# Attention with two MLPs on one core: normalising the value products instead of the exponentials

## The chip, the cores and the metric

One core of a Trainium2 chip runs the whole program. The metric is the device time of one execution in microseconds (us). Engines are named as in the profile: PE (TensorE; PEld its weight loads), DVE (VectorE), ACT (ScalarE), POOL (GpSimd), SP (the engine that issues most transfers).

## The reference

Gated causal attention for 2 batches, 8 heads, 576 positions and 64 columns a head; then a mixture of four experts for all tokens with given probabilities; then a gated MLP.

```python
scores = scale * np.matmul(q, k.transpose(0, 1, 3, 2))
cum = np.cumsum(log_f, axis=-1)
decay = cum[:, :, :, None] - cum[:, :, None, :]
scores = np.where(causal, -1000000000.0, scores + decay)
scores = scores - np.max(scores, axis=-1, keepdims=True)
attn = np.exp(scores)
attn = attn / (np.sum(attn, axis=-1, keepdims=True) + 1e-09)
return np.matmul(attn, v).astype(np.float32)
...
for e in range(E):
    h = np.maximum(x @ w1[e], 0.0)
    out += p[:, e:e + 1] * (h @ w2[e])
...
h = x @ w_in
g = h * (1.0 / (1.0 + np.exp(-1.702 * h)))
return (g @ w_out).astype(np.float32)
```

## The kernel before

The tokens are cut into four chunks: chunk 0 is the first 256 positions of batch 0, chunk 1 its last 320, chunks 2 and 3 the same of batch 1. Attention makes a chunk's 512 columns in four pairs of heads; a chunk of finished columns (x) then goes through the experts, each in two halves, and the MLP. Matmuls of the experts run on a high part (rounded, fp32r) and a low part (the rest): weights are split into `whi` and `wlo`, activations into `xh` and `xl`, and three products are summed.

The attention of a chunk runs over units. In chunk 0 (called plain) a unit is one head with both of its tiles of 128 queries, in plain fp32; in the other chunks it is one tile of 128 queries (or the last 64) for both heads of a pair, with split keys and queries. There are 8 units in chunk 0, 12 in chunk 1 (three a pair), and 8 and 12 in chunks 2 and 3, 40 in all. `attention()` is a generator that emits one step at each pull; a step emits stage by stage: the scores of unit i and their maximum, the exponential and the normalisation of unit i-1, the transposes of unit i-2, and, where a pair has ended, the value product and the splitting of its output at three units behind.

- `emit_max` (L411) adds the decay to the scores, writes them to `e` in SBUF on DVE and takes the row's extreme `mx`. `emit_exp` (L444) is ACT's exponential in place, with the row's sum in `sm`.
- `emit_norm` (L451) adds 1e-9 and takes the reciprocal on DVE (one or two columns, L454 and L455), and multiplies each tile of exponentials by it on POOL (L457, 72 instructions).
- `emit_tr` (L460) transposes `e` on PE into PSUM (L475); ACT, or DVE in chunk 0, copies the result to `ph`.
- `emit_pv` (L489) multiplies the values with `ph` into PSUM, the two heads of a pair in lanes 0 to 63 and 64 to 127 (L505). `emit_x2` (L507) rounds that to `xh` on ACT and subtracts to `xl` on DVE (L514).

Keys, queries and values of a pair are loaded by `load_heads` (L319), one pair ahead; POOL rounds and subtracts them (L337, L338, L346, L347) three units before they are used, and adds the mask to broadcasts of the cumulated decay, `cb` and `cbs` (L349 on). Their pools have three buffers each.

While attention goes on, the main loop takes expert work for the chunks that are done, and pulls attention steps between groups of matmuls so that a chunk is ready when it is needed. `emit_first` does the first layer of chunk 0 as its columns come. The instructions are emitted in program order, and the scheduler of the language, which models time, sets the final order on each engine; engines then run their instructions strictly in order. After the last attention step `begin_late` (L269) closes the attention's pools, and DVE converts the MLP's weights (`mlp_convert`) beside the experts.

Of the kernel before, what the change touches and what calls it, by code (L numbers as in the profile page):

```python
# [15 lines left out]
NT = B * S  # L16
# [17 lines left out]
def attn_moe_mlp(ctx: ExitStack, tc: tile.TileContext, qk0, qk1, qk2, v0, vp, fg, dp, wa_moe, wb_moe, wa_mlp, wb_mlp, outT):  # L34
# [8 lines left out]
    def pool(name, bufs, space=None, scope=ctx):  # L43
        kw = {} if space is None else {"space": space}
        return scope.enter_context(tc.tile_pool(name=name, bufs=bufs, **kw))

    def f(ap):
        return ap.bitcast(F32)
# [32 lines left out]
    att_scope = ctx.enter_context(ExitStack())  # L81
    ac = pool("ac", 1, scope=att_scope)
    hi_p = pool("hi", 2, scope=att_scope)
    qhi_p = pool("qhi", 3, scope=att_scope)
    kq_p = pool("kq", 3, scope=att_scope)
    v_p = pool("v", 3, scope=att_scope)
    cb_p = pool("cb", 4, scope=att_scope)
    cbs_p = pool("cbs", 2, scope=att_scope)
    e_p = pool("e", 3, scope=att_scope)
# [159 lines left out]
        dpb[e] = t  # L249

    def load_probabilities():
        raw = const.tile([128, NT // 32], F32, name="dpraw")
        nc.sync.dma_start(out=raw, in_=dp)
        return raw

    def make_probabilities(raw):

        out = const.tile([128, 4, NT // 128], F32, name="dpn")
        s = const.tile([128, NT // 128], F32, name="dps")
        v = raw.rearrange("p (j e) -> p e j", e=4)  # L260
        nc.gpsimd.tensor_add(s, v[:, 0], v[:, 1])
        for e in (2, 3):
            nc.gpsimd.tensor_add(s, s, v[:, e])
        nc.gpsimd.tensor_scalar(out=s, in0=s, scalar1=1e-9, scalar2=1.0, op0=ALU.add, op1=ALU.mult)
        nc.vector.reciprocal(out=s, in_=s)
        nc.gpsimd.tensor_mul(out, v, s.unsqueeze(1).to_broadcast([128, 4, NT // 128]))
        nc.sync.dma_start(out=dpT.rearrange("e (p j) -> p e j", p=128), in_=out)
# [51 lines left out]
    def load_heads(p, h0):  # L319

        cs, b, s0 = p
        st = pairs[p, h0] = {}
        src = (qk2 if b else qk1)[h0 // 2]
        st["kq"] = kq_p.tile([128, KW], F32, tag="kq", name="kq")
        nc.sync.dma_start(out=st["kq"], in_=src[:, :KW])
        for i, c in enumerate(cs):
            st["q", c] = kq_p.tile([128, QW], F32, tag="qr", name="qr")
            nc.sync.dma_start(out=st["q", c], in_=src[:, KW + i * QW:KW + i * QW + QW])
        st["vd"] = v_p.tile([128, 5, 2, D], F32, tag="vd", name="vd")
        nc.sync.dma_start(out=st["vd"], in_=vp[b * H // 2 + h0 // 2].rearrange("p (t g d) -> p t g d", t=5, g=2))  # L330

# [119 lines left out]
    def emit_norm(c, u):  # L451
        e, sm, todo = sc[c, u]
        k = len(todo)
        nc.vector.tensor_scalar(out=sm[:, 1, :k], in0=sm[:, 0, :k], scalar1=1e-9, scalar2=None, op0=ALU.add)  # L454
        nc.vector.reciprocal(out=sm[:, 0, :k], in_=sm[:, 1, :k])  # L455
        for i, (q0, off, w, _) in enumerate(todo):
            nc.gpsimd.tensor_scalar(out=e[:, off:off + w], in0=e[:, off:off + w], scalar1=sm[:, 0, i:i + 1],  # L457
                                    scalar2=1.0, op0=ALU.mult, op1=ALU.mult)

    def emit_tr(c, u):  # L460

        hs, tiles = u
        s0 = CH[c][1]
        e, sm, todo = sc.pop((c, u))
        for h in hs:
            if (c, h) not in ph_of:
                ph_of[c, h] = pt_p.tile([128, 4, SB], F32, tag="ph", name="ph")
        for k, (q0, off, w, _) in enumerate(todo):
            o = q0 - s0
            nk = (w + 127) // 128  # L470

            for k0, k1 in [(0, min(nk, 4))] + [(4, 5)] * (nk > 4):
                pt = ps_t.tile([128, 512], F32, tag="t", name="t")
                for i in range(k0, k1):
                    nc.tensor.transpose(pt[:, 128 * (i - k0):128 * (i - k0) + 128], e[:, off + 128 * i:off + 128 * i + 128], ident)  # L475
                cols = pt[:, :128 * (k1 - k0)].rearrange("p (i q) -> p i q", q=128)
                for j, h in enumerate(hs if w == S else hs[k:k + 1] if len(hs) > 1 else hs):
                    r = 64 if w == S else 128
                    ph = ph_of[c, h]
                    ph = ph[:, 3:4, 0:64] if k0 else ph[:, 0:k1, o:o + r]  # L480
                    if plain(c) and k1 == 2:
                        nc.vector.tensor_copy(ph, cols[:, :, j * r:(j + 1) * r])
                    else:
                        round_act(ph, cols[:, :, j * r:(j + 1) * r])
# [22 lines left out]
    def emit_x2(c, h):  # L507
        n = CH[c][2]
        if h % 2 == 1:
            k = h // 2  # L510
            x = xf.pop((c, k))[:, :n]
            x_made[0] += 1
            round_act(xh[c][:, k, :], x)
            nc.vector.tensor_sub(xl[c][:, k, :], x, f(xh[c][:, k, :]))  # L514

    STAGES = dict(scores=0, max=0, exp=1, norm=1, tr=2, pv=3, x2=3)
    L_X2 = STAGES["x2"]
# [5 lines left out]
    def attention():  # L523
# [17 lines left out]
        for i in range(len(seq) + L_X2 + 1):  # L541
# [5 lines left out]
                prep_queries(*k)  # L547
            for k in new:
                prep_cum(*k)
            for k in names:  # L550
                j = i - STAGES[k]
                if k in per_unit:
# [268 lines left out]
```

## Time and profile before

| | |
|---|---|
| median of 3 runs | 731.88 us (731.81 to 733.29) |
| the profiled execution's own time | 733.77 us |
| its span in the trace | 732.0 us, mean granted clock 0.998 |
| PE busy | 710.5 us, 97% |
| DVE busy | 457.1 us, 62% |
| POOL busy | 295.1 us, 40% |
| ACT busy | 266.7 us, 36% |

The shares over the whole span hide that the program has stages: attention for chunk 0 alone at first, then attention beside experts, and from some 222 us on experts and MLP without attention. They are read by stretches of the span. PE's busy time counts a matmul from its start to a modelled end, so a waiting matmul can look busy; the time of the weight loads (PEld) is the second view of the same engine. A chain of waits is followed backward from its last instruction, and its shares say on which engine's work the end of the stretch waited.

### The profile page before, as it was taken

How to read it: one execution, taken by the hardware profiler on the slowest of the kernel's cores; microseconds unless marked ns; L12 is line 12 of the kernel's file. 1: busy time of each engine (PE TensorE's matmuls, PEld its weight loads, DVE VectorE, ACT ScalarE, POOL GpSimd, SP SyncE). 2: the span in 40 equal slices, each digit the busy share in tenths (PEclk: the TensorE clock that was granted, in tenths of full speed). 3: DMA queues.
4: the chain of work that ended last, by engine and by line, in shares of the span. 5: the costliest groups of instructions: out<-in, count | busy, mean ns of one | idle time of the engine just before them, and what ended most of it. 6: DMA issues, size and time to landing. Idle time of an engine off the chain costs nothing.

```text
span 732.0 us, 11991 instructions
## 1 busy us (share of the span) xinstructions
PE 710.5 (97%) x4488; PEld 681.7 (93%) x4488; DVE 457.1 (62%) x1023; ACT 266.7 (36%) x629; POOL 295.1 (40%) x377
## 2 busy tenths in 40 slices
PE   4988999999999999999999999999999999999998
PEld 3577889999999999999998999999999999999997
DVE  4765767577748999999999542345962124424422
ACT  4445655566642233222221221223354433333320
POOL 5997896774422022332232432232462222222220
PEclk9999999999999999999999999999999999999999
DMA  8866744332125555454344200000100000000012
GB/s 269 248 194 210 213 162 137 118 103 87 59 90 193 154 193 160 162 173 117 114 144 115 87 30 30 1 1 1 58 0 1 1 1 1 1 0 1 1 44 86
DMA packets 31225, 68.81 MB, mean 94 GB/s; under 512 B 3224, under 2 KB 4768, under 8 KB 31168
## 3 DMA queue, kind: packets, MB, share of 16 engines
q1 hardware_dynamic: 31120, 68.01, 29.6%
q8 instruction: 35, 0.57, 0.3%
q14 instruction: 22, 0.18, 0.1%
q10 hardware_dynamic: 48, 0.05, 0.0%
HBM read 65.62 MB, written 2.41 MB: 93 GB/s over the span
## 4 chain that ended last, share of the span: by engine, by line
PE 84%; POOL 7%; DMA 5%; issue 2%; DVE 1%; SPq 1%; ACT 0%; POOLq 0%; DVEq 0%
PE m L625 39%; PE m L581 39%; PE s L408 2%; POOL e L457 2%; PE x L505 2%; DMA kq<-in_qk_dram 2%; PE t L475 2%; DMA qr<-in_qk_dram 2%; POOL klo L338 1%; POOL qlo L347 1%; POOL cb L360 1%; DMA kd<-fr 1%; POOL cb L363 1%; POOL khi L51 1%; POOL qhi L51 1%
## 5 line engine op out<-in xcount | busy, mean ns | idle before, releaser
L641 POOL TENSOR_TENSOR acc<-acc,tmp 128x384 f32<-128x384 f32 (+3 forms) x112 | 111.9, 1010 | 237.4 <-DVE tmp L639 237.0
L625 PE MATMUL m<-hh,wlo 128*128 128x384 f32 (+2 forms) x640 | 127.7, 320 | 0.9 <-DVE wlo L165 0.9
L625 PE MATMUL m<-hh,whi 128*128 128x384 f32 (+2 forms) x640 | 128.4, 320 | 0.0
L625 PE MATMUL m<-hl,whi 128*128 128x384 f32 (+2 forms) x640 | 128.3, 319 | 0.0
L581 PE MATMUL m<-xh,whi 128*128 128x384 f32 (+2 forms) x624 | 125.7, 321 | 2.2 <-POOL whi L51 2.2
L581 PE MATMUL m<-xh,wlo 128*128 128x384 f32 (+2 forms) x624 | 125.4, 321 | 0.0
L581 PE MATMUL m<-xl,whi 128*128 128x384 f32 (+2 forms) x624 | 125.1, 320 | 0.0
L54 ACT ACTIVATE whi<-wst 128x512 fp32r<-128x512 f32 x103 | 64.8, 630 | 117.6 <-PE m L581 65.9
L625 PEld LDWEIGHTS m<-hh,whi 128*128 128x128 f32 x640 | 106.0, 189 | 1.7 <-issue 0.8
L625 PEld LDWEIGHTS m<-hh,wlo 128*128 128x128 f32 x640 | 105.8, 189 | 1.7 <-DVE wlo L165 1.6
L581 PEld LDWEIGHTS m<-xh,whi 128*128 128x128 f32 x624 | 103.7, 188 | 3.2 <-POOL whi L51 2.5
L625 PEld LDWEIGHTS m<-hl,whi 128*128 128x128 f32 x640 | 106.2, 189 | 0.2
L165 DVE TENSOR_TENSOR wlo<-wst,whi 128x512 fp32r<-128x512 f32 x112 | 90.4, 810 | 25.1 <-ACT whi L54 12.6
L581 PEld LDWEIGHTS m<-xl,whi 128*128 128x128 f32 x624 | 104.0, 188 | 0.2
L581 PEld LDWEIGHTS m<-xh,wlo 128*128 128x128 f32 x624 | 103.8, 188 | 0.3 <-DVE wlo L165 0.2
L616 POOL TENSOR_TENSOR hl<-tmp,hh 128x384 fp32r<-128x384 f32 x48 | 49.1, 1025 | 133.2 <-ACT hh L54 133.2
L607 ACT ACTIVATE hh<-m 128x384 fp32r<-128x384 f32 (+2 forms) x112 | 48.8, 437 | 116.1 <-PE m L581 115.0
L608 DVE SCALAR_TENSOR_TENSOR hl<-m,hh 128x384 fp32r<-128x384 f32 (+2 forms) x112 | 54.8, 492 | 32.3 <-ACT hh L607 32.2
L639 DVE TENSOR_TENSOR tmp<-m,dpb 128x384 f32<-128x384 f32 (+2 forms) x80 | 40.8, 511 | 34.3 <-PE m L625 28.3
L614 DVE TENSOR_TENSOR tmp<-m,sg 128x384 f32<-128x384 f32 x48 | 26.6, 554 | 54.2 <-ACT sg L613 54.2
L448 ACT ACTIVATE e<-e,mx 128x128 f32<-128x128 f32 (+4 forms) x72 | 42.0, 584 | 43.1 <-DVE mx L434 39.3
L457 POOL TENSOR_SCALAR e<-e,sm 128x128 f32<-128x128 f32 (+4 forms) x72 | 46.1, 650 | 21.7 <-DVE sm L455 17.1
(93 smaller groups left out, 771.7 us busy)
## 6 DMA issues: line engine op xcount, KB each, us to landing
wst<-in_wa_moe_dram SPq DMA_DIRECT2D x28, 512.0 KB, 4.6
wst<-in_wb_moe_dram SPq DMA_DIRECT2D x28, 512.0 KB, 4.0
mst<-in_wa_mlp_dram SPq DMA_DIRECT2D x16, 512.0 KB, 3.5
mst<-in_wb_mlp_dram SPq DMA_DIRECT2D x16, 512.0 KB, 3.8
cb<-cumd SPq DMA_DIRECT2D x16, 256.0 KB, 6.1
qr<-in_qk_dram SPq DMA_DIRECT2D x12, 256.0 KB, 3.7
kq<-in_qk_dram SPq DMA_DIRECT2D x8, 352.0 KB, 7.0
vd<-in_vp_dram SPq DMA_DIRECT2D x8, 320.0 KB, 3.7
```

The lines of the kernel that those rows point to most:

```text
L54: nc.scalar.activation(out=out, in_=in_, func=AF.Copy)
L165: sub = nc.vector.tensor_sub(lf, raw, f(hf))
L448: nc.scalar.activation(out=e[:, off:off + w], in_=e[:, off:off + w], func=AF.Exp, scale=-1.0, bias=mx, accum_out=sm[:, 0, k:k + 1])
L457: nc.gpsimd.tensor_scalar(out=e[:, off:off + w], in0=e[:, off:off + w], scalar1=sm[:, 0, i:i + 1], scalar2=1.0, op0=ALU.mult, op1=ALU.mult)
L581: nc.tensor.matmul(p[:, :n], lhsT=w[:, k, :], rhs=x[c][:, k, :], start=(j == 0 and k == 0), stop=(j == 2 and k == 3))
L607: nc.scalar.activation(out=hh[:, g, :n], in_=p[:, :n], func=AF.Relu)
L608: nc.vector.scalar_tensor_tensor(out=hl[:, g, :n], in0=p[:, :n], scalar=0.0, in1=f(hh[:, g, :n]), op0=ALU.max, op1=ALU.subtract)
L614: nc.vector.tensor_mul(t[:, :n], p[:, :n], s[:, :n])
L616: nc.gpsimd.tensor_sub(hl[:, g, :n], t[:, :n], f(hh[:, g, :n]))
L625: nc.tensor.matmul(p[:, :n], lhsT=w[:, k, :], rhs=x[:, k, :n], start=(j == 0 and k == 0), stop=(j == 2 and k == 3))
L639: nc.vector.tensor_mul(t[:, :n], p[:, :n], d)
L641: nc.gpsimd.tensor_add(a, a, t[:, z])
```

## The change

The exponentials are no longer multiplied by their reciprocal sums. Instead `emit_norm` writes each reciprocal, broadcast over 64 columns for each head, into a tile `rec`. With the last transposes of a pair, `emit_rec` transposes `rec` on PE into the same PSUM tile, so that every lane of a head holds the reciprocals along the queries, and ACT copies them to `rt`, which has one buffer. `emit_x2` multiplies the value product by `rt` on DVE into `xt`, and splits that; the subtraction to `xl` goes from DVE to POOL for chunks 1 to 3. Values are loaded by a function of their own at the pair's first unit. Keys and values have two buffers instead of three, and the small tiles of the probabilities live in a temporary.

```diff
+    xt_p = pool("xt", 2, scope=att_scope)
+    rec_p = pool("rec", 2, scope=att_scope)
...
-    v_p = pool("v", 3, scope=att_scope)
+    v_p = pool("v", 2, scope=att_scope)
...
-        st["kq"] = kq_p.tile([128, KW], F32, tag="kq", name="kq")
+        st["kq"] = kq_p.tile([128, KW], F32, tag="kq", name="kq", bufs=2)
...
+    def load_values(p, h0):
+
+        b = p[1]
+        st = pairs[p, h0]
         st["vd"] = v_p.tile([128, 5, 2, D], F32, tag="vd", name="vd")
...
     def emit_norm(c, u):
         e, sm, todo = sc[c, u]
         k = len(todo)
+        h = u[0][0]
+        if (c, h // 2) not in rec:
+            rec[c, h // 2] = rec_p.tile([128, 3, 2, 64], F32, tag="rec", name="rec")
+        r = rec[c, h // 2]
+        r = r[:, :2, h % 2, :] if plain(c) else r[:, (todo[0][0] - CH[c][1]) // 128]
         nc.vector.tensor_scalar(out=sm[:, 1, :k], in0=sm[:, 0, :k], scalar1=1e-9, scalar2=None, op0=ALU.add)
-        nc.vector.reciprocal(out=sm[:, 0, :k], in_=sm[:, 1, :k])
-        for i, (q0, off, w, _) in enumerate(todo):
-            nc.gpsimd.tensor_scalar(out=e[:, off:off + w], in0=e[:, off:off + w], scalar1=sm[:, 0, i:i + 1],
-                                    scalar2=1.0, op0=ALU.mult, op1=ALU.mult)
+        nc.vector.reciprocal(out=r, in_=sm[:, 1, :k].unsqueeze(2).to_broadcast([128, 2, 64]) if k == 2 else
+                             sm[:, 1, 0:1].unsqueeze(2).to_broadcast([128, 2, 64]))
+
+    rec, rcp = {}, {}
+
+    def emit_rec(c, h, pt, o):
+
+        r = rec.pop((c, h // 2))
+        n = CH[c][2]
+        for j in range(0, n, 128):
+            nc.tensor.transpose(pt[:, o + j:o + j + 128], r[:, j // 128].rearrange("p g d -> p (g d)"), ident)
+        t = rcp[c, h // 2] = xt_p.tile([128, SB], F32, tag="rt", name="rt", bufs=1)
+        round_act(t[:, :n], pt[:, o:o + n])
+        if n > 256:
+            round_act(t[64:, 256:n], pt[64:, o + n:o + n + 64])
...
+                if k + 1 == len(todo) and hs[-1] % 2 and k1 == nk and q0 + 128 >= s0 + CH[c][2]:
+                    emit_rec(c, hs[0], pt, 128 * (k1 - k0))
...
-            x = xf.pop((c, k))[:, :n]
+            p, r = xf.pop((c, k)), rcp.pop((c, k))
             x_made[0] += 1
+            x = xt_p.tile([128, SB], F32, tag="xt", name="xt")[:, :n]
+            nc.vector.tensor_mul(x, p[:, :n], r[:, :n])
             round_act(xh[c][:, k, :], x)
-            nc.vector.tensor_sub(xl[c][:, k, :], x, f(xh[c][:, k, :]))
+            (nc.vector if plain(c) else nc.gpsimd).tensor_sub(xl[c][:, k, :], x, f(xh[c][:, k, :]))
...
+            for k in nxt:
+                if first[k] == i:
+                    load_values(*k)
```

POOL's order when the first units of chunk 0 are on their way, before (`kq` and `qr` are the raw keys and queries of the first pair of chunk 1, `e` the exponentials of chunk 0):

```order
L51 TENSOR_SCALAR khi<-kq 128x704
L457 TENSOR_SCALAR e<-e,sm 128x128
L457 TENSOR_SCALAR e<-e,sm 128x256
L51 TENSOR_SCALAR qhi<-qr 128x256 x2
L338 TENSOR_TENSOR klo<-kq,khi 128x704
L457 TENSOR_SCALAR e<-e,sm 128x128
L457 TENSOR_SCALAR e<-e,sm 128x256
L347 TENSOR_TENSOR qlo<-qr,qhi 128x256 x2
```

and with the change:

```order
L51 TENSOR_SCALAR khi<-kq 128x704
L51 TENSOR_SCALAR qhi<-qr 128x256 x2
L346 TENSOR_TENSOR klo<-kq,khi 128x704
L355 TENSOR_TENSOR qlo<-qr,qhi 128x256 x2
L264 TENSOR_TENSOR dpraw<-dpraw 128x9
```

The multiplications of the exponentials are gone from between the splitting of keys and queries, and the probabilities follow at once.

DVE's order where the last pair of chunk 0 is split and the first pair of chunk 1 has its maxima taken (L434, later L442, over the scores `s` with the decay `cbs`), before:

```order
L454 TENSOR_SCALAR sm<-sm 128x2
L434 ISA e,mx<-s,cbs,mx 128x288
L434 ISA mx 128x1
L455 RECIPROCAL sm<-sm 128x2
L454 TENSOR_SCALAR sm<-sm 128x1
L455 RECIPROCAL sm<-sm 128x1
L514 TENSOR_TENSOR xl<-x,xh 128x256
```

and with the change:

```order
L467 TENSOR_SCALAR sm<-sm 128x2
L442 ISA e,mx<-s,cbs,mx 128x288
L442 ISA mx 128x1
L468 RECIPROCAL rec<-sm 128x128
L467 TENSOR_SCALAR sm<-sm 128x1
L540 TENSOR_TENSOR xt<-x,rt 128x256
L468 RECIPROCAL rec<-sm 128x128
L542 TENSOR_TENSOR xl<-xt,xh 128x256
```

The reciprocals stand where they stood, with 128 columns instead of 2 and 1, and the multiplication `xt` has come between them.

PE's order around the last tile of the second pair of chunk 1 (`t<-identr,e` are transposes of exponentials, `m` the experts' products, `s` scores), before:

```order
L625 MATMUL m<-hl,whi 128x256 x4
L475 MATMUL t<-identr,e 128x128 x5
L625 MATMUL m<-hh,whi 128x256 x4
L625 MATMUL m<-hh,wlo 128x256 x4
L408 MATMUL s<-khi 128x288
```

and with the change:

```order
L612 MATMUL m<-xl,whi 128x256 x2
L499 MATMUL t<-identr,e 128x128 x5
L478 MATMUL t<-identr,rec 128x128 x2
L612 MATMUL m<-xh,whi 128x256 x4
L612 MATMUL m<-xh,wlo 128x256 x4
L612 MATMUL m<-xl,whi 128x256 x4
L416 MATMUL s<-khi,qhi 128x512
L416 MATMUL s<-khi,qlo 128x512
L416 MATMUL s<-klo,qhi 128x512
L478 MATMUL t<-identr,rec 128x128
```

The transposes of the reciprocals (L478) follow those of the exponentials, the third one some matmuls later, and the expert that runs beside them is another layer.

## Rows read from the trace of the kernel before

**Rows 1.** Stretches (us): length, busy time of PE, PEld, DVE, ACT, POOL.

```profile
10.00:44.00 34.00, 31.08 (x111) 19.83 (x112) 23.07 (x87) 15.36 (x54) 28.55 (x55) 0.95 0.80 254
44.00:104.00 60.00, 55.68 (x430) 49.48 (x429) 40.50 (x120) 35.77 (x96) 53.07 (x74) 1.00 0.68 209
104.00:222.00 118.00, 118.00 (x866) 108.61 (x868) 75.18 (x227) 65.51 (x180) 66.77 (x98) 1.00 0.32 104
222.00:402.00 180.00, 179.58 (x1207) 178.00 (x1203) 174.55 (x336) 44.94 (x89) 48.02 (x44) 1.00 0.48 151
402.00:732.00 330.00, 326.14 (x1880) 325.82 (x1880) 140.24 (x251) 101.51 (x205) 94.83 (x96) 1.00 0.06 19
```

**Rows 2.** Waits of PE, whole span: us in total, times, longest.

```profile
PE s L408 <- DMA kd<-fr: 10.2, 1, 10.2
PE t L475 <- POOL e L457: 3.3, 4, 2.2
```

**Rows 3.** Chain of waits, 0 to 106 us: shares by engine and line.

```profile
by line: POOL e L457 15.4%; DMA kq<-in_qk_dram 12.4%; DMA qr<-in_qk_dram 12.0%; issue 11.1%; POOL klo L338 6.3%; POOL qlo L347 5.7%; POOL cb L360 5.4%; DMA kd<-fr 5.2%; POOL cb L363 4.1%; POOL khi L51 4.0%; POOL qhi L51 3.7%; POOL cbs L369 
```

**Rows 4.** Normalisation on POOL, L457, by stretch: length, POOL busy (instructions).

```profile
10.00:44.00 34.00, 7.76 (x18) 0.95 0.80 254
44.00:104.00 60.00, 15.85 (x19) 1.00 0.68 209
104.00:222.00 118.00, 22.45 (x36) 1.00 0.32 104
```

**Rows 5.** Groups by form, 0 to 225 us, POOL: busy us, mean ns.

```profile
L641 POOL TENSOR_TENSOR acc<-acc,tmp 128x320 f32<-128x320 f32 x8 | 9.3, 1159 | 13.3 <-DVE tmp L639 13.2
L641 POOL TENSOR_TENSOR acc<-acc,tmp 128x256 f32<-128x256 f32 x12 | 8.8, 738 | 1.9 <-DVE tmp L639 1.8
```

**Rows 6.** The same view, DVE: maxima over 256 and 128 columns.

```profile
L434 DVE CUSTOM_DVE_ANT_0 e<-s,cb 128x256 f32<-128x256 f32 x16 | 6.7, 417 | 1.6 <-PE s L408 1.1 <-PE t L475 0.5
...
L434 DVE CUSTOM_DVE_ANT_0 e<-s,cb 128x128 f32<-128x128 f32 x16 | 4.4, 283 | 1.6 <-PE s L408 1.1 <-POOL e L457 0.5
```

**Rows 7.** Reciprocals: two groups by form, and L455's durations (ns min/median/max).

```profile
L455 DVE RECIPROCAL sm<-sm 128x2 f32<-128x2 f32 x32 | 5.3, 164 | 1.0
...
L265 DVE RECIPROCAL dps<-dps 128x9 f32<-128x9 f32 x1 | 0.2, 204 | 0.0
...
L455 DVE RECIPROCAL sm<-sm x40: 148/166/167, 13.1 to 201.8; 128x2 f32<-128x2 f32 x32, 128x1 f32<-128x1 f32 x8
```

**Rows 8.** Additions before the reciprocals, L454: by form, then DVE busy by stretch.

```profile
L454 DVE TENSOR_SCALAR sm<-sm 128x2 f32<-128x2 f32 x32 | 12.1, 380 | 8.9 <-ACT e L448 8.9
...
L454 DVE TENSOR_SCALAR sm<-sm 128x1 f32<-128x1 f32 x8 | 1.2, 152 | 5.2 <-ACT e L448 5.2
...
10.00:44.00 34.00, 4.17 (x10) 0.95 0.80 254
44.00:104.00 60.00, 3.12 (x11) 1.00 0.68 209
104.00:222.00 118.00, 6.07 (x19) 1.00 0.32 104
```

**Rows 9.** Groups by form, DVE: subtraction to xl.

```profile
L514 DVE TENSOR_TENSOR xl<-x,xh 128x320 fp32r<-128x320 f32 x7 | 3.4, 485 | 5.1 <-ACT xh L54 5.1
...
L514 DVE TENSOR_TENSOR xl<-x,xh 128x256 fp32r<-128x256 f32 x8 | 3.3, 414 | 1.7 <-ACT xh L54 1.7
```

**Rows 10.** Timeline of PE near 204 us: start, length, instructions.

```profile
204.35 1.04 PE L475 MATMUL t<-identr,e 128*128 128x128 f32 x8
205.14 0.82 PE L581 MATMUL m<-xh,whi 128*128 128x320 f32 x4
```

**Rows 11.** Groups by form, ACT: rounding the value product.

```profile
L54 ACT ACTIVATE xh<-x 128x320 fp32r<-128x320 f32 x8 | 3.5, 434 | 11.9 <-PE x L505 11.7
```

**Rows 12.** Waits of POOL, 28 to 104 us: total, times, longest.

```profile
POOL cbs L369 <- DMA cbs<-cumd: 7.1, 4, 4.2
```

**Rows 13.** Timeline of PE near 402 us.

```profile
402.51 0.97 PE L625 MATMUL m<-hh,wlo 128*128 128x384 f32 x4 [0.72 <-DVE wlo L165]
```

More of the change, by code (lines that the diff above doesn't have):

```diff
@@ L251, in load_probabilities, with make_probabilities @@
     def load_probabilities():
[L252 to L260, printed above, removed]
+        t = tmp_p.tile([128, WN], F32, tag="tmp", name="dpraw")
+        nc.sync.dma_start(out=t[:, :NT // 32], in_=dp)
+        return t
+    def make_probabilities(t):
+        w = NT // 32
+        out = t[:, w:2 * w].rearrange("p (e j) -> p e j", e=4)
+        s = t[:, 2 * w:2 * w + NT // 128]
+        v = t[:, :w].rearrange("p (j e) -> p e j", e=4)
         nc.gpsimd.tensor_add(s, v[:, 0], v[:, 1])
```

## Prediction

> **What bounds the kernel now.** I read the stretches first, then TensorE's waits, then the chain of waits, then the groups by line. In the stretches [rows 1] the reader is to see that TensorE is busy for all of 118.00 us from 104 to 222 us, for 179.58 of 180 from 222 to 402 and for 326.14 of 330 after that. Whatever the change takes off another engine there is worth nothing by itself, and every instruction added to TensorE costs its own time. Before 104 us TensorE has gaps: 31.08 busy of 34 us (stretch A, 10 to 44) and 55.68 of 60 us (stretch B, 44 to 104). Its weight loads, which are padded less by waiting, give 49.48 of 60 in B, so the gap of B lies between 60 - 55.68 = 4.3 and 60 - 49.48 = 10.5 us. GpSimd is the busiest of the others there: 28.55 of 34 (84%) and 53.07 of 60 (88%). Of TensorE's waits with a name [rows 2], one is for the first data (10.2 us, untouched) and 3.3 us, 2.2 of it in one piece, are for the normalised exponentials. The chain up to 106 us [rows 3] runs through GpSimd, and its largest entry is the normalisation, L457: 15.4% of 106 = 16.3 us. So the change takes away the work that leads this chain; the question is what is late next.
>
> **What it removes.** The 72 normalising multiplications of GpSimd: 7.76 us in A, 15.85 in B, 22.45 in C (104 to 222) [rows 4]. In C that is worth 0, since TensorE has no gap. In A and B GpSimd falls to 28.55 - 7.76 = 20.8 and to 53.07 - 15.85 = 37.2 us. In B it gets four subtractions back (the low half of the attention output), at most 1.16 us each by the GpSimd rows of the same two sizes [rows 5]: 41.9 of 60. GpSimd is then late no more.
>
> **What it puts on VectorE.** (1) Every reciprocal now writes 128 columns a lane, not 1 or 2. No row has that shape, so it is bounded. Below: if the reciprocal went at the pace of the other VectorE operations, whose 128 and 256 column forms take 283 and 417 ns [rows 6], 1.05 ns a column, it would take 0.164 + 126 x 0.00105 = 0.30 us. From its own rows: 2 columns take 164 ns, the one of 9 columns takes 204 [rows 7]: 40 ns for 7 columns, 5.7 ns each, so 0.164 + 126 x 0.0057 = 0.88 us. Above: from the shortest one (148 ns) to the 204 it is 8.0 ns a column, 1.16 us. I take 0.88, the only slope that comes from two reciprocals, and keep 0.30 and 1.16. Less the 0.16 that it took, each adds 0.72 us; there are 10 in A, 11 in B and 19 in C by the count of the additions in front of them [rows 8]. (2) The 16 multiplications of the value product have the operands of the subtraction of L514, one from PSUM and one from SBUF, so its 414 and 485 ns [rows 9]. In A four are added, 1.7 us; in B and C each takes the place of a subtraction that goes to GpSimd, so 0. (3) The additions of two columns took 380 ns against 152 for one column [rows 8]; a column doesn't cost 228 ns, they stand behind GpSimd. With GpSimd's share down I let them all take 152: 4.17 - 10 x 0.152 = 2.65 us back in A, 3.12 - 11 x 0.152 = 1.45 in B. Bounds of that: 0 and these.
>
> VectorE's sum: in A 23.07 + 7.2 + 1.7 - 2.65 = 29.3 us, in B 40.50 + 7.9 - 1.45 = 47.0. In A that is more than GpSimd had. If VectorE leads there with the 84% that GpSimd reached, A lasts 29.3 / 0.84 = 34.8 us: **A costs 0.8 us**, and TensorE's 2.2 us wait for the normalisation becomes one for VectorE. In B, at GpSimd's 88%, it would last 47.0 / 0.884 = 53.1 us, a gain of 6.9; TensorE's own gap allows 4.3 to 10.5. I take the middle of 4.3 and 6.9: **B gives 5.6 us**. In C VectorE has 75.18 + 19 x 0.72 = 88.9 of 118 us: covered by TensorE; if that cover failed, up to 0.88 us for each of the 8 head pairs there, 7 us.
>
> [...]
>
> **What it puts on TensorE.** 40 more transposes of 128 x 128: 8 in A, 12 in B, 20 in C. Eight in a row hold TensorE from 204.35 to 205.14 us [rows 10], 0.10 us each. In A they lie in gaps; **B pays 1.2, C pays 2.0 us**. They stand right behind the transposes of the last tile of a pair, and queued behind them in TensorE's order are scores, value products and MoE matmuls, so a late reciprocal holds all of these. The waits for that in A and B are in the pace above; in C I take 0: the normalisation, at 22.45 / 36 = 0.62 us a piece and mostly two pieces a unit, left TensorE without a gap there [rows 1, 4].
>
> **What it puts on ScalarE.** 16 copies of the transposed reciprocals at no more than 434 ns [rows 11] and 12 smaller ones: some 2 us in A, 3 in B, on 15.36 of 34 and 35.77 of 60 us: nothing while VectorE and TensorE have more. The single buffer of that copy makes ScalarE wait for the multiplication of the pair before, which is three units old by then. The last pair's path to the first expert is longer by a multiplication and by the slower subtraction on GpSimd, about 1.2 us; the first matmuls on it need the high half alone, so 0.
>
> **What moves on the queue.** Value loads leave their place ahead of the next key loads and are issued at a pair's first unit; their pieces are wanted three units later. Two buffers for keys: the buffer asked for was split into its halves one pair before, so 0. GpSimd waited 7.1 us in 28 to 104 us for one broadcast, 4.2 of it once [rows 12]; the order on SP puts fewer bytes ahead of it. I count nothing for that; bounds 0 and 4.2 us gained. The probabilities' small tiles move into a temporary that nobody wants so early: 0. After 222 us VectorE is busy 174.55 of 180 us [rows 1] and TensorE waits for it by 0.72 us at 402 us [rows 13]; both come earlier or later together, so 0, and at worst 1.5 us if VectorE starts later there by the longer last path.
>
> **Sum.** A +0.8, B -5.6 + 1.2, C +2.0, the rest 0: -1.6 us on the profiled execution's 733.77, so 732.2; that execution lies 1.89 above the median, which puts the forecast at **730.3 us**. About 0.2% (1.5 us) is what a measurement of this kernel can tell from no change.
>
> **Rivals.** *Cheap reciprocals.* At 0.30 us VectorE has 23.5 us in A and 40.6 in B and leads nowhere. A then gives the 2.2 us wait, B the middle of TensorE's own bounds, 7.4 - 1.2, C costs 2.0: -6.4, so 725.5 us, and at the far ends (2.9 and 10.5) 721.7. For it: TensorE is then the only full engine. Against it: the two reciprocal rows.
> *Reciprocals lead (slower).* At 1.16 us A has 23.07 + 10.0 + 1.7 - 2.65 = 32.1 us, at 84% 38.2: +4.2. B has 50.1, at 88% 56.6: -3.4 + 1.2. C +2.0. Together +4.0: 735.9 us, and without the relief of the additions (2.65 and 1.45 us, each over its pace) 740.7. Between 0.88 and 1.16 us the sum goes from -1.6 to +4.0, so it turns at about 0.96 us for one reciprocal. For it: VectorE works in order, and in A the next unit's maxima stand behind the reciprocal. Against it: B's gap.
> *Late broadcasts.* If the 4.2 us wait of GpSimd in B stays whole, B gives 5.6 - 4.2 - 1.2 = 0.2 only: +2.6, so 734.5 us. For it: the wait is for a transfer, which a freer GpSimd doesn't hasten. Against it: fewer bytes lie ahead on SP. That the change doesn't do what it says can be left out: the orders show GpSimd without the 72 multiplications.
>
> **How the numbers follow.** Forecast 0.40 (727.5 to 732.0 us; 0.25 of it faster, 0.15 the same). Cheap reciprocals 0.20, faster. Late broadcasts 0.12 (0.04 the same, 0.08 slower). Reciprocals lead 0.28, slower. So faster 0.45, the same 0.19, slower 0.36. The range goes from 723, inside the cheap case, to 738.5, inside the slower one; the far ends of both, about 2 in 10, are left out.
>
> **What would show it.** In the changed profile: the reciprocal's mean (0.88, under 0.96 for a gain); VectorE near 29 us where the first chunk ends, and that end 0 to 1 us later than before; TensorE's first fully busy stretch beginning 3 to 5 us before 104 us; 40 transposes worth 4 us, with no wait for a reciprocal after that point. Wrong would be a reciprocal far from 0.88, TensorE waiting for the transposed reciprocals in C, or the cbs wait of GpSimd unchanged.

## The result, and the profile after

The changed kernel took 742.98 us in the median of 4 runs (739.73 to 743.45), beside 732.59 us (731.81 to 733.65) for the kernel before: a ratio of 1.0131, 95% interval 1.0098 to 1.0164. It is slower by 1.3%, where 730.3 us was forecast and the range ended at 738.5. The profiled execution has a span of 741.1 us, 9.1 more than before.

The stretches of the changed kernel, which answer to [rows 1]; the columns are length, then busy time of PE, PEld, DVE, ACT, POOL, the granted clock, the DMA share and GB/s:

```profile
10.00:44.00 34.00, 32.51 (x134) 23.75 (x135) 29.95 (x85) 16.97 (x59) 24.51 (x44) 1.00 0.80 259
44.00:104.00 60.00, 56.40 (x411) 46.55 (x410) 44.57 (x121) 37.00 (x104) 35.20 (x51) 1.00 0.59 189
104.00:222.00 118.00, 118.00 (x852) 108.06 (x852) 89.46 (x230) 68.54 (x183) 51.13 (x70) 1.00 0.35 102
222.00:402.00 180.00, 177.75 (x1212) 175.85 (x1211) 168.65 (x324) 46.94 (x96) 43.83 (x43) 1.00 0.49 152
402.00:732.00 330.00, 329.15 (x1897) 328.22 (x1896) 148.35 (x263) 102.16 (x206) 99.66 (x100) 1.00 0.07 20
```

GpSimd is relieved as planned: 35.20 us in stretch B against 53.07. TensorE got little from it, 56.40 busy us against 55.68, and it did fewer instructions in them (411 against 430). The waits of PE in the changed kernel, which answer to [rows 2], and the chain of waits up to 106 us, which answers to [rows 3]:

```profile
PE s L416 <- DMA kd<-fr: 9.8, 1, 9.8
PE s L416 <- DVE mx L442: 3.6, 3, 2.0
PE m L612 <- DVE hl L639: 2.2, 2, 1.1
PE m L633 <- POOL whi L51: 1.4, 1, 1.4
PE m L656 <- DVE wlo L167: 0.8, 1, 0.8
```

```profile
by line: DMA cbs<-cumd 16.8%; DMA kq<-in_qk_dram 10.2%; PE s L416 8.0%; PE x L531 6.9%; DMA wst<-in_wb_moe_dram 6.0%; PE m L612 5.6%; DMA kd<-fr 5.3%; PE t L499 4.7%; PE m L656 4.7%; DMA cb<-cumd 4.6%; DVE e L442 3.9%; DVE wlo L167 3.5%; DV
```

The wait for normalised exponentials is gone, and a wait for the row maxima stands in its place. The normalisation's 15.4% of the chain has gone to a transfer: the broadcast `cbs` of the cumulated decay has 16.8% of it. GpSimd's waits from 28 to 104 us show the same (the row answers to [rows 12]: 17.3 us, where it waited 7.1):

```profile
POOL cbs L377 <- DMA cbs<-cumd: 17.3, 4, 6.9
```

How that reaches TensorE is seen in the timeline of the changed kernel near 56 us, rows of GpSimd, then VectorE, then TensorE (start, length, instruction; in brackets the idle time before it and what ended that):

```profile
56.41 0.71 POOL L377 TENSOR_TENSOR cbs<-cbs,tri 64x64 f32<-64x64 f32 x2 [6.92 <-DMA cbs<-cumd]
57.20 0.62 POOL L51 TENSOR_SCALAR whi<-wst 128x512 fp32r<-128x512 f32 x1
...
57.86 0.69 DVE L167 TENSOR_TENSOR wlo<-wst,whi 128x512 fp32r<-128x512 f32 x1 [2.50 <-POOL whi L51]
58.47 0.42 DVE L639 SCALAR_TENSOR_TENSOR hl<-m,hh 128x256 fp32r<-128x256 f32 x1
58.80 0.68 DVE L442 CUSTOM_DVE_ANT_0 e<-s,cb 128x512 f32<-128x512 f32 x1
...
59.55 0.40 PE L416 MATMUL s<-khi 128*128 128x288 f32 x1 [0.58 <-DVE mx L442]
```

(`L377` is the addition of the mask to the broadcast, `whi` a weight half, `wlo` its rest, `e` with `mx` a maximum, `s` scores.) GpSimd waits 6.92 us for the broadcast; the weight half `whi` stands behind that; VectorE waits 2.50 us for `whi`, with the maxima behind it; TensorE's next scores wait for a maximum. The chain comes again at 71 us (GpSimd waits 4.80 us) and at 89 (3.53 us); the last ends in TensorE's longest wait for a maximum, 2.03 us at 91.45.

GpSimd comes to this wait 6.4 us earlier than before, the broadcast only 3.6. The same broadcast in the kernel before, its issue and its first use, and then its issue in the changed kernel (the use there is at 56.41, above):

```profile
47.24 0.51 SPq L366 DMA_DIRECT2D cbs<-cumd  x1
60.03 0.70 POOL L369 TENSOR_TENSOR cbs<-cbs,tri 64x64 f32<-64x64 f32 x2 [4.18 <-DMA cbs<-cumd]
```

```profile
45.20 0.51 SPq L374 DMA_DIRECT2D cbs<-cumd  x1
```

It is issued 2.0 us earlier, and used 11.2 us after its issue, where it was 12.8. Before, GpSimd began to wait at 60.03 - 4.18 = 55.85 us, with the change at 56.41 - 6.92 = 49.49.

**Where the 9.1 us lie.** Waiting matmuls can look busy, so I worked out TensorE's lost time from the counts of instructions by form: elapsed time, less each instruction done so far at one price for all kernels. The prices are distances from start to start in gapless rows: 0.173 us for 384 columns, 0.147 for 320, 0.120 for 256, 0.134 for 288, 0.233 for 512, 0.10 for a transpose [rows 10], 0.11 for a value product, 0.23 per 128 columns of the plain fp32 scores (0.22 in the row of four at 29.64 us in the kernel before). What is wrong in a price falls out of a comparison once both kernels have done the same matmuls; before the end it is an estimate. Lost time up to each point, in us; the last column leaves out the same 4.3 us at the end of every span, and kernels with the 40 transposes do 4.0 us more work on top (e2 and the others are the runs of the next section):

| kernel | to 44 | to 104 | to 222 | to the end | added work |
|---|---|---|---|---|---|
| before | 23.1 | 31.1 | 36.1 | 38.1 | 0 |
| changed | 20.7 | 31.2 | 38.1 | 43.2 | 4.0 |
| e2_no_norm | 19.6 | 29.9 | 34.4 | 37.8 | 0 |
| e3_loads_only | 21.8 | 31.3 | 42.3 | 46.8 | 0 |
| e7_neutral_before | 21.2 | 30.4 | 38.7 | 40.6 | 0 |
| p4_nonorm_loads | 20.5 | 28.3 | 32.2 | 36.6 | 0 |
| e8_no_transposes | 18.1 | 27.5 | 32.9 | 35.0 | 0 |
| q1_nonorm_tr40 | 19.2 | 29.5 | 33.0 | 39.3 | 4.0 |
| q2_after_unread | 19.2 | 25.9 | 33.3 | 37.6 | 4.0 |

The changed kernel loses 43.2 - 38.1 = 5.1 us more and works 4.0 us more: 9.1, the difference of the spans. By stretch, with 8, 12 and 17 transposes in A, B and C and 3 after 222 us: A is 20.7 - 23.1 + 0.8 = -1.6 us; B 10.5 - 8.0 + 1.2 = +3.7; C 6.9 - 5.0 + 1.7 = +3.6; after 222 us 5.1 - 2.0 + 0.3 = +3.4.

### The profile page after: what moved, and what is told of

It is laid out like the page before. It is cut to its first block, busy times and chain, and to the rows that moved or that the text cites. A ratio compares the mean times of both kernels' runs of the same rounds, so it can differ in the third digit from the quotient of the medians.

```text
span 741.1 us, 11958 instructions
## 1 busy us (share of the span) xinstructions
PE 719.7 (97%) x4528; PEld 688.0 (93%) x4528; DVE 486.0 (66%) x1027; ACT 275.3 (37%) x653; POOL 258.8 (35%) x317
## 4 chain that ended last, share of the span: by engine, by line
PE 77%; DVE 10%; DMA 9%; issue 2%; POOL 1%; SPq 0%; ACT 0%; DVEq 0%; POOLq 0%
PE m L656 35%; PE m L612 33%; PE s L416 3%; PE x L531 3%; DMA cbs<-cumd 2%; PE t L499 2%; DVE wlo L167 2%; DMA kq<-in_qk_dram 1%; DMA mst<-in_wb_mlp_dram 1%; DVE cvd L230 1%; DVE hl L639 1%; DMA mst<-in_wa_mlp_dram 1%; DVE wf L224 1%; DVE cvt L216 1%; DMA wst<-in_wb_moe_dram 1%
## 5 line engine op out<-in xcount | busy, mean ns | idle before, releaser
L670 DVE TENSOR_TENSOR tmp<-m,dpb 128x384 f32<-128x384 f32 (+2 forms) x80 | 40.8, 511 | 32.0 <-PE m L656 29.3
L167 DVE TENSOR_TENSOR wlo<-wf,whi 128x512 fp32r<-128x512 f32 x32 | 26.6, 830 | 27.6 <-ACT whi L54 26.6
## 6 DMA issues: line engine op xcount, KB each, us to landing
kq<-in_qk_dram SPq DMA_DIRECT2D x8, 352.0 KB, 10.3
```

Source lines behind the costliest of these rows:

```text
L167: sub = nc.vector.tensor_sub(lf, raw, f(hf))
L670: nc.vector.tensor_mul(t[:, :n], p[:, :n], d)
```

## The experiments

Each ran in three rounds beside the kernel before, whose median was 732.4 to 734.4 us in the five groups of runs; ratios are to that, with their 95% interval, and differences of medians between groups carry that spread. The groups did not all run on one chip, so a difference of a few us between medians of two groups is an estimate. I had three theories to begin with, and they are named by number in the first expectations: the first laid the loss to the long reciprocals, the second to TensorE's own new work and the order that it leads to, the third to the loads and the two buffers. Whether GpSimd's relief had been worth anything was to be seen beside them. A theory S, of the scheduler's order, came after these runs.

### The first three theories: reciprocals, normalisation, loads

Two runs made the reciprocal of the changed kernel as short as it was, in two columns at most, and let ScalarE or GpSimd write it to 128 columns. In `emit_norm` (the second has a multiplication by 1 on GpSimd in place of the last line):

```
-        nc.vector.reciprocal(out=r, in_=sm[:, 1, :k].unsqueeze(2).to_broadcast([128, 2, 64]) if k == 2 else
...
+        nc.vector.reciprocal(out=sm[:, 0, :k], in_=sm[:, 1, :k])
+        ri = sm[:, 0, :k].unsqueeze(2).to_broadcast([128, 2, 64]) if k == 2 else sm[:, 0, 0:1].unsqueeze(2).to_broadcast([128, 2, 64])
+        round_act(r, ri)
```

> The changed kernel, but VectorE takes the reciprocal of 1 or 2 columns again and ScalarE writes it out to the 128 columns of rec. Theory 1, the 128 column reciprocals hold up VectorE and through it TensorE: VectorE loses some 40 x 0.79 = 31 us before 222 us, and of the 10.4 us that the change costs all but the 4 us of the 40 transposes comes back: 735 to 738 us. Theory 2, the cost is TensorE's own new work and the order it leads to: 741 to 744 us, as with the change. Theory 3, the loads with two buffers: no difference from the change either.

> As the run before, but GpSimd writes the reciprocal out to the 128 columns: 40 multiplications of 128 columns, at 0.43 us some 17 us, where the kernel before had 46 us of normalisation. Theory 1: 735 to 738 us, if GpSimd has that room. Theories 2 and 3: 741 to 744 us.

Measured: 741.35 us (1.0093, 1.0065 to 1.0121) and 741.31 us (1.0096, 1.0069 to 1.0122). Against the changed kernel's 1.0131 (1.0098 to 1.0164) the intervals overlap: what the short reciprocals bring back is 0.35 to 0.38% by the two ratios, and not clear of noise. The second has a wait of its own, of TensorE for the tile `rec` that GpSimd now writes, so it doesn't measure the reciprocals alone:

```profile
PE t L479 <- POOL rec L470: 5.6, 4, 3.1
```

What the long ones cost on VectorE itself, in the changed kernel (answers to [rows 7]; count, durations in ns as min/median/max, first and last start in us):

```profile
L468 DVE RECIPROCAL rec<-sm x40: 936/952/954, 12.9 to 202.7; 128x128 f32<-128x128 f32 x40
```

Two groups by form of the same kernel, the additions before the reciprocals (answers to [rows 8]) and the larger of GpSimd's subtractions to `xl` (busy us, mean ns; then idle time before them):

```profile
L467 DVE TENSOR_SCALAR sm<-sm 128x2 f32<-128x2 f32 x32 | 11.2, 351 | 6.5 <-ACT e L456 6.3
...
L542 POOL TENSOR_TENSOR xl<-xt,xh 128x320 fp32r<-128x320 f32 x8 | 8.4, 1054 | 19.3 <-ACT xh L54 19.3
```

The next kernel is the one before without the normalisation; the results stay unscaled.

```
-        for i, (q0, off, w, _) in enumerate(todo):
-            nc.gpsimd.tensor_scalar(out=e[:, off:off + w], in0=e[:, off:off + w], scalar1=sm[:, 0, i:i + 1], ...)
```

> The kernel before without its 72 normalising multiplications; this leaves the normalisation out of the attention, everything else stays. It shows the most that freeing GpSimd can give. If GpSimd led the first 104 us, as the chain says: 722 to 728 us. If VectorE, TensorE and the transfers are right behind it: 730 to 732 us, and then the change had nothing to win from the start.

Measured: 731.48 us (0.9970, 0.9947 to 0.9992). To take all 46 us off GpSimd, with nothing in their place, is worth 0.3%. Its stretch B:

```profile
44.00:104.00 60.00, 55.53 (x410) 47.98 (x408) 40.37 (x125) 36.16 (x99) 34.00 (x51) 0.97 0.67 203
```

The waits of PE and of POOL in that stretch:

```profile
PE s L408 <- DVE mx L434: 4.5, 2, 3.2
...
POOL cbs L369 <- DMA cbs<-cumd: 18.5, 3, 8.1
```

TensorE is no busier than before (55.53 against 55.68), GpSimd waits 18.5 us for broadcasts, where [rows 12] has 7.1 in a longer stretch, and TensorE waits for maxima; around and behind the wait of 3.2 us, which ends at 85 us, its granted clock is 0.69 from 84 to 88 us and 0.78 to 90. By the table the kernel is 3.5 us ahead at 44 us, 1.2 at 104 and 0.3 at the end (its profiled execution was the slowest of its seven). In B it loses 10.3 us, and the other kernels of the table without normalisation on GpSimd and without transposes, e8 and p4, lose 9.4 and 7.8, where the kernel before loses 8.0 and the forecast's 5.6 us would have left 2.4. So the gain that the forecast drew from GpSimd's relief in B isn't there to be had.

Then the loads of the change alone, in the kernel before: two buffers for keys and values, and values loaded at the pair's first unit.

```
-    v_p = pool("v", 3, scope=att_scope)
+    v_p = pool("v", 2, scope=att_scope)
-        st["kq"] = kq_p.tile([128, KW], F32, tag="kq", name="kq")
+        st["kq"] = kq_p.tile([128, KW], F32, tag="kq", name="kq", bufs=2)
+            for k in nxt:
+                if first[k] == i:
+                    load_values(*k)
```

> The kernel before with the change's loads alone: two buffers for keys and for values, values loaded at the pair's first unit. Theory 3, the loads make the broadcasts late: 735 us or more. Theories 1 and 2: within 2 us of the kernel before, 731 to 734 us.

Measured: 742.26 us (1.0097, 1.0070 to 1.0125). Most of its loss is one event: the table has 11.0 us lost from 104 to 222 where the kernel before has 5.0. The timeline of this kernel, TensorE, then GpSimd, then the issue on SP:

```profile
107.76 1.33 PE L480 MATMUL t<-identr,e 128*128 128x128 f32 x5 [6.05 <-POOL e L462]
...
106.16 0.70 POOL L374 TENSOR_TENSOR cbs<-cbs,tri 64x64 f32<-64x64 f32 x2 [3.78 <-DMA cbs<-cumd]
106.96 0.74 POOL L462 TENSOR_SCALAR e<-e,sm 128x576 f32<-128x576 f32 x1
...
95.99 1.07 SPq L371 DMA_DIRECT2D cbs<-cumd  x1
```

The broadcast is issued at 95.99 and lands at 106.16, GpSimd waits for it, the normalisation stands behind that wait, and TensorE stands 6.05 us for the normalisation.

### The loads, edit by edit, and the order

> The kernel before with one edit: the keys of a pair have two buffers instead of three; values keep three and are loaded where they were. The loads taken over whole cost 7 to 9 us. Theory K, the key buffers carry it: a load of keys then waits on SP for the low half of the pair before, and the broadcasts, values and weights behind it on that queue wait too: 738 to 741 us beside some 733. Theory V, the values carry it: 732 to 734. Theory S, any such edit makes the scheduler put the instructions in another order, and the order is what costs: somewhere between 731 and 742 with no sum over the parts.

> The kernel before with one edit: two value buffers instead of three, loaded where they were. Theory K: 732 to 734 us, no change. Theory V by the buffers: the load of values then waits for the value product of two pairs before, with the broadcasts and the next keys behind it on SP: 738 to 741. Theory S: anything from 731 to 742.

> The kernel before with one edit: the values of a pair are loaded by a function of their own at the pair's first unit; three buffers of keys and of values stay. Theory K: 732 to 734 us. Theory V by the place: the load comes later than weights and broadcasts and the value product or the order around it is late: 738 to 741. Theory S: anything from 731 to 742; the three single edits then don't add up to the 7 to 9 us of all three together.

> The changed kernel with one part undone: the values are loaded with the keys of their pair again, one pair ahead; two buffers of each stay. If the late place of the values costs what the loads cost (7 us): 733 to 736 us, level with the kernel before. If the key buffers or the reciprocals cost it: 740 to 743, as the changed kernel.

Each is a part of the last diff (the last one takes the `load_values` lines out of the changed kernel). Measured: two key buffers 742.33 us (1.0113, 1.0098 to 1.0128); two value buffers 739.97 (1.0081, 1.0063 to 1.0099); late values 737.41 (1.0048, 1.0032 to 1.0063); the changed kernel with early values 750.11 (1.0214, 1.0186 to 1.0241). The single edits cost 3.8 to 8.7 us and all three together 7.9, so they don't add; and late values, which cost alone, save 7 us in the changed kernel. The cost of the last one shows early: its granted clock is 0.80 from 10 to 44 us, where the changed kernel has 1.00, and TensorE waits 8.4 us for maxima. That speaks for theory S: the scheduler makes another order of each edit, and the order costs. To see how much, one small edit, meant to be neutral, went into both kernels:

```
+    round_pool(tri, mask[:, 128:])
     load_heads(passes[1], 0)
     for _ in range(2):
         load_pair()
-    round_pool(tri, mask[:, 128:])
-    dp_raw = load_probabilities()
+        dp_raw = load_probabilities()
     for _ in range(2):
         load_pair()
```

> The kernel before with one neutral edit: the one rounding of the mask to tri, which GpSimd does once near the start, stands ahead of the first key loads in the program instead of behind them. No buffer, no load, no instruction is other; but the scheduler's order changes from TensorE's 40th row on. Theory S (the order costs, whatever the edit): 736 to 743 us beside some 733, as after the single edits of the buffers. Theory B (fewer buffers and late loads cost as such): 732 to 735.

> The changed kernel with the same neutral edit (the rounding to tri ahead of the first key loads). Theory S: anything from 736 to 750 us, away from the changed kernel's 743 by more than 2. Theory B: 742 to 744.

Measured: 736.74 us (1.0064, 1.0049 to 1.0079) and 746.58 us (1.0197, 1.0176 to 1.0218). The edit makes the kernel before 4.3 us slower, and the changed one 3.6. But it isn't neutral, as the expectations take it to be: besides the move of the rounding, the load of the probabilities (18 KB) has come into the loop and is issued twice. The row of e7_neutral_before, which in the kernel before has one:

```profile
L253 SPq DMA_DIRECT2D dpraw<-in_dp_dram x2: 467/792/1117, 10.5 to 14.6; - x2
```

So the runs show that a very small edit is worth some 4 us here; how much of that is the order, and how much the second load on the queue, they don't tell apart. A difference of some 4 us between two of these kernels can't be put down to what an edit is about, and that part of it is the loss of an order that suits the kernel before is likely and not shown.

### The transposes

First the subtraction to `xl` back on VectorE, in the changed kernel:

```
-            (nc.vector if plain(c) else nc.gpsimd).tensor_sub(xl[c][:, k, :], x, f(xh[c][:, k, :]))
+            nc.vector.tensor_sub(xl[c][:, k, :], x, f(xh[c][:, k, :]))
```

> The changed kernel with the subtraction to xl back on VectorE for all chunks, as before. If GpSimd's subtractions hold the experts of the next chunk (their 25 to 34 us of waiting on the high half are with broadcasts behind them): 739 to 741 us. If they cost nothing: 742 to 744.

Measured: 744.0 us (1.0172, 1.0151 to 1.0192): nothing there. Then the changed kernel without its transposes; ScalarE copies the untransposed tile, so the scale is wrong:

```
-        for j in range(0, n, 128):
-            nc.tensor.transpose(pt[:, o + j:o + j + 128], r[:, j // 128].rearrange("p g d -> p (g d)"), ident)
...
-        round_act(t[:, :n], pt[:, o:o + n])
+        r = r.rearrange("p j g d -> p (j g d)")
+        round_act(t[:, :n], r[:, :n])
```

> The changed kernel without the 40 transposes of the reciprocals: ScalarE copies the untransposed tile in their place, so the values are scaled by the wrong reciprocals; all else stays. If a transpose costs the 0.10 us of the forecast: 4 us less, 739. If it costs more where it stands (only two or three in a row between other matmuls), 0.15 us: 737. If the order decides: away from both by some us.

Measured: 730.42 us (0.9968, 0.9953 to 0.9984), 12.6 us under the changed kernel: more than any of the expectations. Long reciprocals, copies, multiplications, GpSimd's subtractions and the loads are all in it, and together with GpSimd's relief they leave it 0.3% under the kernel before, as e2 is. The next four runs tell transposes, loads and order apart. The transposes alone, in the kernel before, of the identity and read by nobody:

```
+                if k + 1 == len(todo) and hs[-1] % 2 and k1 == nk and q0 + 128 >= s0 + CH[c][2]:
+                    for j in range(128 * (k1 - k0), 128 * (k1 - k0) + CH[c][2], 128):
+                        nc.tensor.transpose(pt[:, j:j + 128], ident, ident)
```

> The kernel before with 40 transposes added at the places where the changed kernel has them (of the identity, into the same spare columns; nobody reads them), nothing else. By the price of 0.10 us each, all on the path: 4 us more, 736 to 738. If transposes cost three times that where they stand: 743 to 746. If only the order matters: 736 to 743, not to be told from the first.

Measured: 745.32 us (1.0159, 1.0128 to 1.0189), 12.4 us more for 4 us of work. Of its loss, a part is again the normalisation held up on GpSimd; the wait of PE in this kernel:

```profile
PE t L475 <- POOL e L457: 10.2, 8, 3.5
```

The edit of e7, with its second load, in the kernels without transposes and without normalisation:

> The changed kernel without its 40 transposes (the wrong scale, as in e8_no_transposes) and with the neutral move of the tri rounding. If the transposes themselves cost 12 us: 729 to 733, the lead stays. If e8 had a lucky order: 734 to 740.

> The kernel before without the normalisation (left out, not replaced) and with the neutral move of the tri rounding. If GpSimd's relief makes the kernel less sensitive to the order: 730 to 733. If its 731.5 was a lucky order: 734 to 740.

Measured: 731.47 us (0.9971, 0.9952 to 0.9990) and 735.22 us (1.0023, 1.0011 to 1.0035). The first keeps its lead; against the changed kernel with the same edit, 746.58, that is 15.1 us for the transposes. The second loses 3.7 us, and has one long wait of TensorE for a maximum:

```profile
81.03 0.77 PE L408 MATMUL s<-khi,qhi 128*128 128x512 f32 x1 [9.32 <-DVE mx L434]
```

The chain that ends there has 12.16 us of a broadcast `cb` in it: a late broadcast can cost without any normalisation behind it. And the loads without the normalisation:

> The kernel before with the loads of the change (two key and two value buffers, values late) and without the normalisation (left out). If the loads cost by a normalisation that stands behind a broadcast's wait on GpSimd: that is gone, 731 to 734 us. If they cost by themselves, the 7 to 9 us of the loads stay: 739 to 741. By the order alone: anywhere between.

Measured: 732.26 us (0.9989, 0.9970 to 1.0008). The loads, which cost 7.9 us with the normalisation, cost 0.8 without it (against the 731.48 of e2; 1.4 by the ratios). Its stretches B and C:

```profile
44.00:104.00 60.00, 57.78 (x429) 50.83 (x428) 39.12 (x128) 39.09 (x106) 37.55 (x54) 0.97 0.65 208
104.00:222.00 118.00, 118.00 (x873) 109.56 (x872) 76.10 (x229) 62.94 (x171) 43.28 (x60) 1.00 0.35 106
```

The waits of PE in it from 44 to 112 us:

```profile
PE s L413 <- DVE mx L439: 2.2, 1, 2.2
```

The 6 us event of e3 near 104 us is gone with the normalisation that stood behind the broadcast. So the loads need not slow a kernel that has no normalisation, as the changed one; e8, which has them too, says the same.

Last, whether the transposes themselves or the chain through them cost the 12 us: the same 40 unread transposes in the kernel without normalisation, and in the changed kernel in place of its own.

> The kernel before without the normalisation (left out, not replaced) and with 40 transposes of the identity at the places of the changed kernel, which nobody reads. If transposes cost their price: 4 us above the 731.5 to 735.2 without them, 735.5 to 739. If they cost what the variants differ by: 742 to 746.

> The changed kernel with its 40 transposes replaced by 40 of the identity that nobody reads; ScalarE copies the untransposed reciprocals, so the scale is wrong; all else as changed. If the transposes cost it: 742 to 744, as the changed kernel. If the chain through them costs it: 734 to 736, which is 4 us above the variant without any transposes.

Measured: 739.61 us (1.0097, 1.0072 to 1.0122) and 738.08 us (1.0075, 1.0059 to 1.0092). Against the same kernels without them, 731.48 and 730.42, that is 8.1 and 7.7 us for 40 unread transposes, 0.2 us each; the profiled executions of the two pairs are 5.6 and 6.7 us apart. Part of it can be the order, which the added transposes may change too. From the second to the changed kernel, where they are read, it is another 4.9 us. In all, five pairs of kernels differ by the transposes: 7.7, 8.1, 12.4, 12.6 and 15.1 us, each more than the 4.0 us of work.

What goes beyond the 4.0 us shows late in the two pairs with unread transposes. In the profiled executions both have no more lost than their partners at 104 us (29.5 against 29.9, 25.9 against 27.5), and more after 222 us: 6.3 against 3.4, and 4.3 against 2.1; as the changed kernel has 5.1 against 2.0 before. There VectorE converts the MLP's weights (first and last start, from the row of the first of its four steps, in the kernels e8_no_transposes, q2_after_unread and the changed one):

```profile
L216 DVE TENSOR_SCALAR cvt<-mst x32: 410/426/1181, 218.8 to 514.7; 128x512 uint32<-128x512 uint32 x32
```

```profile
L216 DVE TENSOR_SCALAR cvt<-mst x32: 411/427/1124, 223.7 to 521.3; 128x512 uint32<-128x512 uint32 x32
```

```profile
L216 DVE TENSOR_SCALAR cvt<-mst x32: 411/427/1103, 228.7 to 526.8; 128x512 uint32<-128x512 uint32 x32
```

Attention ends later, so the conversion starts later (218.8, 223.7, 228.7; 221.9 in the kernel before), beside experts that need VectorE too; TensorE's 2.2 us wait for `hl` in the changed kernel lies there. But the later start is not borne out as the cause: p4_nonorm_loads, without transposes, starts earlier than the kernel before,

```profile
L214 DVE TENSOR_SCALAR cvt<-mst x32: 411/426/1236, 219.5 to 516.2; 128x512 uint32<-128x512 uint32 x32
```

and loses 4.4 us after 222 us, as e3, also without any, loses 4.5; and p1_tr40, with transposes, starts at 233.0 and loses 3.2 by the same count. What makes this loss stays open.

## Why the prediction was wrong, step by step

**B, -5.6 us: wrong, +2.5.** This is the first step that failed. The pace of B was taken from GpSimd's and VectorE's busy shares, and the relief was given to TensorE up to its gap. TensorE's own waits in B, before, show how little of the gap was the normalisation's:

```profile
PE m L581 <- POOL whi L51: 2.2, 1, 2.2
PE t L475 <- POOL e L457: 1.1, 3, 0.5
```

Only 1.1 us of [rows 2]'s 3.3 lie there; the 2.2 us piece lies in A. The wait behind the relief was the rival "late broadcasts", with 0.12: GpSimd's wait for `cbs` didn't shrink, it grew from 7.1 [rows 12] to 17.3 us, and reached TensorE through `whi`, `wlo` and the maxima. That this is all of the 2.5 us is not shown: p4 has waits of the same size for broadcasts (19.2 us from 28 to 104 us) and loses 7.8 us in B. The run without any normalisation, with no transposes and no long reciprocals to pay, gives the size of what there was to win: 0.3% (0.1 to 0.5) for the whole kernel, and with the edit of e7 nothing.

**Transposes, 0.8 in gaps and 3.2 us paid: 7.7 and 8.1 us unread, and 12.6 with the chain through them.** This is the second failed step, and the larger one. The price of 0.10 us each held as work, but the step took the work as the whole cost; what the rest is made of stays open. The wait for the chain, 0 in the forecast, is the least settled: 4.9 us between q2 and the changed kernel are 5.3 us lost before 104 us, and the small edit of e7 alone is worth about as much. No row of PE names a wait for a transposed reciprocal; ScalarE waits for them 2.0 us in two places.

**After 222 us, 0 and at worst 1.5: 3.4**, 0.3 of it three transposes that come that late. "Both come earlier or later together" was wrong: three kernels with transposes lose 2.2 to 3.1 us more there than their partners, and p1 1.2 more than the kernel before. But e3 and p4, without transposes, lose some 2.5 more than the kernel before too, so this loss isn't tied to them.

**A, +0.8: -1.6.** VectorE has 29.95 us there, as forecast (29.3), and yet led nothing; TensorE lost 2.4 us less in spite of it. A busy share of 84% reached by GpSimd was no limit for VectorE, which has 88% in the changed kernel. The forecast let the 2.2 us wait for the normalised exponentials become one for VectorE; no wait took its place, and a slower clock behind it went too. The wait and the stretch around it before, then the same stretch with the change:

```profile
39.84 0.48 PE L475 MATMUL t<-identr,e 128*128 128x128 f32 x1 [2.19 <-POOL e L457]
39.00:43.00 4.00, 3.16 (x10) 2.06 (x11) 2.05 (x6) 1.07 (x4) 3.49 (x7) 0.59 0.64 144
```

```profile
39.00:43.00 4.00, 4.00 (x25) 3.10 (x24) 3.73 (x9) 2.06 (x6) 3.85 (x8) 1.00 0.83 257
```

Before, the granted clock is 0.50 from 40 to 43 us, behind that wait, and 0.95 over all of A; with the change A has 1.00. By 34 x 0.05 that is an estimated 1.7 us of TensorE's time on top of the 2.2.

**C, +2.0: +3.6.** The 17 transposes that fall there are 1.7 of it; the rest, 1.9, has no wait with a name. That TensorE has no gap there was read from a busy time in which waiting matmuls count: by the count above the kernel before already loses 5.0 us in C. (Of the smaller copies on ScalarE the trace has 8, not 12; nothing hung on them.)

**Reciprocals, 0.88 us: 0.95.** The slope from two short ones was a good guide: (0.950 - 0.164) / 126 = 6.2 ns a column, between the 5.7 and the 8.0 of the bounds. The forecast put the turning point at 0.96, and the measured value just under it, so by its own sum the change should have come out even. That it didn't shows that the reciprocal was not what decided: with short ones, which ScalarE or GpSimd write out, the kernel is still 0.9% slower. The additions, hoped for at 152 ns, are still at 351, so the relief of 2.65 and 1.45 us didn't come; e8, which has them too, is no slower for it. In both kernels those of two columns took 0.16 to 0.17 us where no instruction of GpSimd ran beside them; the longest, 1.65 us at 162.78 us before and 1.53 at 28.30 with the change, ran beside a subtraction of GpSimd to `klo`.

**Loads, 0: right for this kernel as far as p4 and e8 tell, by luck.** e3 and the single edits show a cost of 4 to 9 us in a kernel that has the normalisation on GpSimd, p4 none clear of noise without it. The step looked at the buffers one by one, and not at what stands behind a broadcast's wait.

What is left open: why the transposes cost more than their work, and how the 12.6 us between the changed kernel and the one without transposes divide between the chain through them and the order. No variant that computes everything was faster than the kernel before, and the lower end seen for any is 730.4 us, 0.3% under it: with TensorE busy 97% of the span, there was hardly anything to win here for a change that adds to TensorE's work.

## What to carry to other kernels

Where an engine is to be relieved, first leave its work out altogether, and see what the whole kernel gains: that is a first measure of what a replacement can bring, and here it was 0.3%, against 1.1% for the 40 transposes that the replacement put on the full engine. Before a gain is claimed for an engine that waits in order, look at what the freed time turns into: here a wait for a transfer, with the same successors queued behind it. And where a scheduler sets the order, run a neutral edit too, and look in the trace whether it is neutral: here one rounding moved and one small load doubled made 4 us of difference, as much as some of the effects looked for.

## What the runs showed of the hardware

- A reciprocal of 128 columns takes VectorE 0.95 us, one of two columns 0.164 [rows 7].
- A broadcast of the cumulated decay (576 columns to 128 lanes, 288 KB) took from its issue at 95.99 us to 106.16 in e3, 10 us, on the queue that weights and keys are issued on too; it is the wait that GpSimd's relief turned into.
- 40 unread transposes of 0.10 us each on a full TensorE made two kernels 7.7 and 8.1 us longer by the medians, about twice their work; a part of that can be the order.
- After TensorE had waited 2.19 us, up to 39.84 us in the kernel before, its granted clock was 0.50 from 40 to 43 us. Matmuls of 288 columns then started 0.24 us apart (40.35 to 40.59), and 0.13 us apart at full clock in the changed kernel (42.87 to 43.00).
